# GpSimd's arithmetic in the weight stage moved to VectorE, in an attention and feed-forward kernel on one core

## The chip, the core and the metric

The kernel runs on one core of a Trainium2 chip. A core has engines that each work through their own queue of instructions in order: TensorE (PE in the profile; its weight loads are PEld), VectorE (DVE), ScalarE (ACT), GpSimd (POOL), and SyncE (SP), whose queue only issues transfers here. Engines wait for one another by semaphores. The time is that of one execution on the device in microseconds (us), the median of several.

## The reference

Four batches of 768 positions, 8 heads of width 64, all in fp32. Attention is local: position s sees the 8 first positions and its own last 96, with a bias that falls with distance by a slope per head.

```python
scores = scale * np.matmul(q, k.transpose(0, 1, 3, 2))
keep = is_global | is_local
scores = scores + bias[None, :, :, :]
scores = np.where(keep, scores, -1000000000.0)
a = np.exp(scores - np.max(scores, axis=-1, keepdims=True))
a = a / (np.sum(a, axis=-1, keepdims=True) + 1e-09)
x = np.matmul(a, v)                      # then (3072, 512): heads side by side
h = x @ w_in                             # w_in (512, 2048)
out = (h / (1.0 + np.exp(-h))) @ w_out   # w_out (2048, 512)
```

The two weight matrices come as 64-bit floats, so they are 16 MB in memory.

## The kernel before

**Split numbers.** Products are made from pairs. An fp32 value is rounded to a high part in a shorter format, and its low part is the value less the high part; a product is high x high + high x low + low x high. For the weights the high part is rounded on ScalarE (`conv_hi`, L387) and the low part subtracted (`conv_lo`, L391).

**Weights.** They come in 32 pieces (n = 0 to 31) of 128 partitions x 512 numbers, 512 KB each; even n are a 128-wide column slice of w_in for one f (f = n / 2, 16 in all), odd n the matching rows of w_out. A piece is loaded by SP (`stage`, L364) to a staging buffer. There are three of these; for n under 20 two of every five pieces use space that is lent by the last pieces' own place. Three VectorE steps put the 64-bit float's bits together as an fp32 (`conv1` L368, `conv2` L374, `conv3` L380), after which the staging buffer is free; then come `conv_hi` and `conv_lo`. The fp32 form `wf` has three buffers until `conv_lo` is through.

**Attention.** 24 blocks of 128 positions. Per block, keys and queries are turned by PE, split (L503 and L507, from block 6 on L476 and L487), and the part of the keys that the next block needs is copied on (`carry`, L514 and L516, on GpSimd). Each block has four pairs of heads: scores on PE (L528, later L500), bias and row maximum in one VectorE operation (L540), exponentials with their sum on ScalarE (L548), sum guarded and inverted (L555, L559), exponentials scaled by it (`norm`, L572 or L574), turned on PE (L583), moved to SBUF (L589), and multiplied with the values on PE (L603). The result is split again (L615, L618).

**Feed-forward.** Two blocks make a group of 256 tokens; there are 12 groups, g = 0 to 11. One unit is one (g, f): 12 matmuls with w_in (L723), tanh on ScalarE (L729), the gate on VectorE (L733), its high part on ScalarE (L737), its low part (L742), 6 matmuls with w_out (L749). Groups 0 and 1 run side by side while the weights come in, f after f; from group 2 on every weight is there, and attention of later blocks is mixed between the units.

**The order.** All engines' queues are written out by a planner when the kernel is built (`Plan.run`). Each operation is given to it with its engine, a cost in ns, a rank, what it needs and what buffers it holds. The planner walks through time and gives each engine that is free the lowest rank that is ready and has buffers. The order of every queue follows from these costs, so another engine or cost for one operation moves others too. Where PE would have nothing before a set time, the planner puts in small filler matmuls (L861).

**Which engine.** `conv_lo` is always on GpSimd. The table's `PL=4` puts a gate's low part on GpSimd for groups 0 and 1 and f under 4, eight in all. `NP=(16, 0)` puts the first head's scaling of each of the first 16 pairs of heads on GpSimd; `NA=(0, 0)` puts none on ScalarE. Everything else of these kinds is on VectorE.

Of the kernel before, what the change touches and what calls it, by code (L numbers as in the profile page):

```python
# [10 lines left out]
F32 = mybir.dt.float32  # L11
# [6 lines left out]
ALU = mybir.AluOpType  # L18
# [15 lines left out]

    C0=14, CR=1, LW=1, LB=5, QB=3.5, RI=0.1, RN=0, RP=0.2, RM=0, RV=1.2, RQ=0.1, RB=3, LK=-25, LAG=1,

    BP=(4, 3), NA=(0, 0), NP=(16, 0), PL=4, NX=20, CF=2, AHEAD=5, CN=4, I0=6, QS='ACT',
)


# [130 lines left out]
def attn_moe(ctx, tc, q, k, v, n_global, n_local, w_in, w_out, out):  # L171
    nc = tc.nc
# [3 lines left out]
    NHP = H // 2  # L176
# [52 lines left out]
    st = {}  # L229
# [83 lines left out]
    op = plan.op  # L313
    DVE = lambda n: 1000 * (62 + n) / 960
# [21 lines left out]
    for hp in range(NHP):  # L336
        for first in (True, False):
            p = hp >= PAR["BP"][first]
# [49 lines left out]

    def conv_lo(n):
        _, hi, lo = weights(n)  # L390
        nc.gpsimd.tensor_sub(lo, st["f", n], hi.bitcast(F32))  # L391

    o_w, o_l = [], [None, None]
    for n in range(2 * NFC):
        rank = PAR["C0"] + PAR["CR"] * n
        a, m, x = [] if lent(n) is not None else [Buf("big")], Buf("mid"), lent(n)
        o = op("DMA", 1456, rank - PAR["LW"], (lambda n=n: stage(n, "w")), [o_l[x]] if not a else (), a, PAR["DL"])
        o = op("DVE", 335, rank, (lambda n=n: conv1(n)), [o], [*a, m])
        o = op("DVE", 602, rank, (lambda n=n: conv2(n)), [o], [*a, m])
        o = op("DVE", 602, rank, (lambda n=n: conv3(n)), [o], [*a, m])  # L400
        if x is not None:
            o_l[x] = o
        o_wf = o
        hi = op("ACT", 520, rank, (lambda n=n: conv_hi(n)), [o] + (o_l if n >= 2 * NFC - 4 else []), [m])
        lo = op("POOL", 1225, rank, (lambda n=n: conv_lo(n)), [hi], [m])
        o_w.append((hi, lo))
    lo["caps"] = dict(pt=5)

# [149 lines left out]
        t = blk[i]  # L558
        nc.vector.reciprocal(t["inv", hp], t["inv", hp])  # L559

    def norm_on(u, a):

        return "ACT" if u < PAR["NA"][a] else "POOL" if u < PAR["NP"][a] else "DVE"

    def norm(i, hp, a):
        t = blk[i]
        x = t["p", hp][:, a, :cols(i)[1]]
        eng = norm_on(NHP * i + hp, a)
        if eng == "ACT":
            nc.scalar.mul(x, x, t["inv", hp][:, a:a + 1])  # L570
        elif eng == "POOL":
            nc.gpsimd.tensor_mul(x, x, t["inv", hp][:, a:a + 1].to_broadcast(x.shape))  # L572
        else:
            nc.vector.tensor_scalar(x, x, t["inv", hp][:, a:a + 1], None, ALU.mult)  # L574

    def turn_p(i, hp, tp):
        t = blk[i]
# [48 lines left out]
    for i in range(B * NJ):  # L626
# [51 lines left out]
        for hp in range(NHP):  # L678
            u = NHP * i + hp
            stacked = i >= PAR["I0"]  # L680
            s, pe, pt, tp = [Buf("s") for _ in range(1 if stacked else 2)], Buf("pe"), Buf("pt"), Buf("tp")
            ks = [kk[x] for x in ("KH", "KL", "QH", "QL") + (("R",) if stacked else ())]
            n = cols(i)[1]
            o = op("PE", 432 if stacked else 640, u,
                   (lambda i=i, hp=hp, s=s, f=stack_scores if stacked else scores: f(i, hp, s)),
                   [x for y, x in ob.items() if i or y[1] <= hp < y[1] + NHP // 2] + [before.get("s") if stacked else None], s + ks)
            before["s"] = o_s[u] = o
            if u == PAR["HU"]:
                o["hold"] = 1
            o_e = []  # L690
            for a in range(2):
                x = op("DVE", 318 if j else 210, u, (lambda i=i, hp=hp, a=a: top_of(i, hp, a)),
                       [o, o_b[j == 0, hp], before.get("top") if stacked and not a else None], [s[a % len(s)], pe])
                if not a:
                    before["top"] = x
                o_e.append(op("ACT", ACT(n, 112) + 186, u, (lambda i=i, hp=hp, a=a: expo(i, hp, a)), [x], [pe]))
            o = op("DVE", 67, u - PAR["RI"], (lambda i=i, hp=hp: guard(i, hp)), o_e, [pe])
            o = op("DVE", 72, u - PAR["RI"], (lambda i=i, hp=hp: inverse(i, hp)), [o], [pe])
            cost = dict(ACT=380, DVE=250, POOL=640) if j else dict(ACT=293, DVE=196, POOL=400)
            o = [op(norm_on(u, a), cost[norm_on(u, a)], u - PAR["RN"], (lambda i=i, hp=hp, a=a: norm(i, hp, a)), [o], [pe])  # L700
                 for a in range(2)]
            o = op("PE", 438 if j else 220, u - PAR["RP"], (lambda i=i, hp=hp, tp=tp: turn_p(i, hp, tp)), o, [pe, tp])
            o_m.append(op("ACT", ACT(512 if j else 256), u - PAR["RM"], (lambda i=i, hp=hp: move_p(i, hp)), [o, before.get("move") if stacked else None], [tp, pt]))
            before["move"] = o_m[-1]
            pts.append(pt)
            if not stacked or hp == NHP - 1:
                last = op("PE", ((1860 if j else 980) if stacked else 540 if j else 290), u - PAR["RV"],
                          (lambda i=i, hp=hp, av=pav: values_of(i, hp, av)),
                          [*o_m, last] + o_v, [*pts, pav, xb[g]["xh"], xb[g]["xl"], kk["vn"]] + ([kk["vp"]] if j else []))
                o_m, pts = [], []  # L710
# [27 lines left out]

    def moe_low(g, f):
        mo["gl", g, f] = gl = sb2.tile([P, GT], F32R, name="gl")  # L740
        eng = nc.gpsimd if g < 2 and f < PAR["PL"] else nc.vector
        eng.tensor_sub(gl, mo["th", g, f], mo["gh", g, f].bitcast(F32))  # L742

    def moe_o(g, f, tt, po):
        gh, gl, po = mo["gh", g, f], mo["gl", g, f], bank(po)
# [25 lines left out]
    for g in range(NGRP):  # L771
# [3 lines left out]
        for f in range(NFC):  # L775
            rank = 1e3 + (max(g, 1) * NFC + f + (PAR["LAG"] + 0.5 if g else 0))
            ph, th, gh, gl = Buf("h"), Buf("th"), Buf("gh"), Buf("gl")
            for c in range(NCC):
                o = op("PE", 329, rank + PAR["LK"] / 10, (lambda g=g, f=f, c=c, h=ph: moe_h(g, f, c, h)),
                       [o, *o_w[2 * f]] + o_x[g], [ph, xb[g]["xh"], xb[g]["xl"]])  # L780
                if f == c == 0:
                    o["hold"] = 2 if g == 1 else 1
            o_h[g, f] = o
            t = op("ACT", 264, FIRST + rank, (lambda g=g, f=f: moe_tanh(g, f)), [o], [ph, th])
            t = op("DVE", 335, FIRST + rank, (lambda g=g, f=f: moe_gate(g, f)), [t], [ph, th])
            hi = op("ACT", 307, FIRST + rank, (lambda g=g, f=f: moe_high(g, f)), [t], [th, gh])
            p = g < 2 and f < PAR["PL"]
            lo = op("POOL" if p else "DVE", 690 if p else 335, FIRST + rank, (lambda g=g, f=f: moe_low(g, f)), [hi], [th, gh, gl])
            for tt in range(NB):
                last[tt] = op("PE", 651, rank, (lambda g=g, f=f, tt=tt, x=po[tt]: moe_o(g, f, tt, x)),  # L790
                              [hi, lo, last[tt], *o_w[2 * f + 1]], [gh, gl, *po[tt:]])
                if g < 2 and f == NFC - 1:
                    last[tt]["hold"] = 1
# [243 lines left out]
```

## Time and profile before

| | |
|---|---|
| median of 3 runs | 757.61 us (755.15 to 757.96) |
| the profiled execution | 757.3 us, its span 755.5 us |
| mean granted TensorE clock | 0.992 |
| busy: PE, DVE, ACT, POOL | 721.3, 491.7, 422.6, 91.6 us |
| GpSimd's low parts of weights, L391 | 32 instructions, 47.5 us |
| GpSimd's scalings, L572 | 16, 9.1 us |
| GpSimd's low parts of gates, L742 | 8, 7.2 us |
| GpSimd's copies of keys, L514 and L516 | 80, 29.5 us |
| weight stage (first to last L368 to L380) | 32.8 to 144.9 us |

A row of the timeline gives the start in us, the length in us, the engine, the line in the kernel, the operation and the tiles (out<-in). Groups give count, busy us, mean ns of one, and the engine's idle time just before them with what ended it. A record's length runs from the start to the end of the instruction on its engine, so time in which it stood still after its start is inside.

### The profile page before, as it was taken

How to read it: one execution, taken by the hardware profiler on the slowest of the kernel's cores; microseconds unless marked ns; L12 is line 12 of the kernel's file. 1: busy time of each engine (PE TensorE's matmuls, PEld its weight loads, DVE VectorE, ACT ScalarE, POOL GpSimd, SP SyncE). 2: the span in 40 equal slices, each digit the busy share in tenths (PEclk: the TensorE clock that was granted, in tenths of full speed). 3: DMA queues.
4: the chain of work that ended last, by engine and by line, in shares of the span. 5: the costliest groups of instructions: out<-in, count | busy, mean ns of one | idle time of the engine just before them, and what ended most of it. 6: DMA issues, size and time to landing. Idle time of an engine off the chain costs nothing.

```text
span 755.5 us, 14215 instructions
## 1 busy us (share of the span) xinstructions
PE 721.3 (95%) x5203; PEld 636.8 (84%) x5203; DVE 491.7 (65%) x1439; ACT 422.6 (56%) x1105; POOL 91.6 (12%) x147
## 2 busy tenths in 40 slices
PE   8997676899999999999999999999999999999996
PEld 6776555788999999999899999998899999998995
DVE  5899999864666656756666757656666756544322
ACT  5976233574656656755656756646656646543221
POOL 3355545400000000000000000000000000000000
PEclk9999899999999999999999999999999999999999
DMA  7785535112412412313313324324314232000000
GB/s 148 214 211 175 163 121 183 56 29 54 132 62 69 118 60 71 102 49 97 99 49 90 87 52 109 85 54 109 97 31 109 71 82 54 29 2 1 29 1 33
DMA packets 117501, 63.98 MB, mean 85 GB/s; under 512 B 93744, under 2 KB 110384, under 8 KB 117424
## 3 DMA queue, kind: packets, MB, share of 16 engines
q1 hardware_dynamic: 116992, 62.86, 30.5%
q8 instruction: 43, 0.70, 0.4%
q14 instruction: 34, 0.28, 0.1%
q10 hardware_dynamic: 432, 0.13, 0.1%
HBM read 56.69 MB, written 6.29 MB: 83 GB/s over the span
## 4 chain that ended last, share of the span: by engine, by line
PE 83%; DVE 12%; issue 3%; DMA 1%; ACT 0%; SPq 0%; DVEq 0%
PE bank L723 33%; PE bank L749 32%; PE bank L603 5%; PE bank L583 4%; PE bank L500 4%; DVE wf L368 3%; PE bank L448 3%; DVE wf L374 2%; DVE wf L380 2%; DVE pe L540 1%; PE bank L861 1%; DVE pe L574 1%; PE bank L528 1%; DVE th L733 1%; DMA qn<-in_q_dram 1%
## 5 line engine op out<-in xcount | busy, mean ns | idle before, releaser
L723 PE MATMUL bank<-xh,WIH 128*128 128x256 f32 x768 | 226.2, 295 | 17.4 <-DVE th L733 16.1
L723 PE MATMUL bank<-xl,WIH 128*128 128x256 f32 x768 | 217.0, 283 | 0.0
L723 PE MATMUL bank<-xh,WIL 128*128 128x256 f32 x768 | 216.0, 281 | 0.0
L723 PEld LDWEIGHTS bank<-xh,WIH 128*128 128x128 f32 x768 | 145.2, 189 | 33.0 <-DVE th L733 22.3
L723 PEld LDWEIGHTS bank<-xl,WIH 128*128 128x128 f32 x768 | 145.4, 189 | 5.8
L723 PEld LDWEIGHTS bank<-xh,WIL 128*128 128x128 f32 x768 | 145.8, 190 | 0.0
L749 PE MATMUL bank<-WOH,gh 128*128 128x512 f32 x336 | 137.6, 410 | 0.0
L749 PE MATMUL bank<-WOH,gl 128*128 128x512 f32 x336 | 134.2, 399 | 2.7 <-DVE gl L742 2.7
L749 PE MATMUL bank<-WOL,gh 128*128 128x512 f32 x336 | 133.1, 396 | 0.0
L729 ACT ACTIVATE th<-bank 128x256 f32<-128x256 f32 x192 | 73.7, 384 | 101.1 <-PE bank L723 98.2
L737 ACT CAST gh<-th 128x256 fp32r<-128x256 f32 x192 | 77.3, 403 | 92.6 <-PE bank L749 55.0
L733 DVE SCALAR_TENSOR_TENSOR th<-th,bank 128x256 f32<-128x256 f32 x192 | 80.3, 418 | 64.4 <-ACT th L729 62.7
L742 DVE TENSOR_TENSOR gl<-th,gh 128x256 fp32r<-128x256 f32 x184 | 80.4, 437 | 54.1 <-ACT gh L737 51.8
L540 DVE CUSTOM_DVE_ANT_0 pe<-bank,B 128x232 f32<-128x232 f32 (+1 forms) x192 | 69.7, 376 | 62.8 <-PE bank L500 54.9
L548 ACT ACTIVATE pe<-pe,NM 128x232 f32<-128x232 f32 (+1 forms) x192 | 90.5, 473 | 22.9 <-DVE NM L540 21.1
L749 PEld LDWEIGHTS bank<-WOH,gl 128*128 128x128 f32 x336 | 63.6, 189 | 21.3 <-DVE gl L742 6.0
L589 ACT COPY pt<-bank 128x512 f32<-128x512 f32 (+1 forms) x96 | 52.4, 549 | 45.2 <-PE bank L583 44.2
L749 PEld LDWEIGHTS bank<-WOL,gh 128*128 128x128 f32 x336 | 64.3, 191 | 6.4
L749 PEld LDWEIGHTS bank<-WOH,gh 128*128 128x128 f32 x336 | 64.3, 191 | 6.3 <-issue 0.3
L514 POOL CAST KH<-KH 128x32 fp32r<-128x32 f32 x20 | 4.5, 227 | 458.5 <-PE bank L500 449.9
L583 PE MATMUL bank<-ident,pe 128*128 128x128 f32 (+1 forms) x352 | 55.3, 275 | 3.5 <-DVE th L733 2.5
L574 DVE TENSOR_SCALAR pe<-pe,rs 128x232 f32<-128x232 f32 (+1 forms) x176 | 53.9, 342 | 1.1
(112 smaller groups left out, 1008.2 us busy)
## 6 DMA issues: line engine op xcount, KB each, us to landing
c<-in_moe_w_in_dram SPq DMA_DIRECT2D x16, 512.0 KB, 4.0
c<-in_moe_w_out_dram SPq DMA_DIRECT2D x16, 512.0 KB, 4.3
vn<-in_v_dram SPq DMA_DIRECT2D x24, 256.0 KB, 3.4
w<-in_moe_w_in_dram SPq DMA_DIRECT2D x12, 512.0 KB, 4.8
w<-in_moe_w_out_dram SPq DMA_DIRECT2D x12, 512.0 KB, 3.6
kn<-in_k_dram SPq DMA_DIRECT2D x23, 256.0 KB, 3.0
qn<-in_q_dram SPq DMA_DIRECT2D x23, 256.0 KB, 3.2
out_dram<-osb SPq DMA_DIRECT2D x23, 256.0 KB, 3.2
```

Of the source, the lines that this page charges most:

```text
L540: nc.vector.tensor_tensor_reduce(t["p", hp][:, a, :n], t["s", hp][a][:, :n], B1[:, h] if i % NJ else B0[:, h], -SC, 3.0e38, ALU.add, ALU.m ...
L548: nc.scalar.activation(x, x, AF.Exp, bias=NM[:, i * H + h:i * H + h + 1], scale=-1.0, accum_out=t["sum", hp][:, a:a + 1],)
L574: nc.vector.tensor_scalar(x, x, t["inv", hp][:, a:a + 1], None, ALU.mult)
L583: nc.tensor.transpose(ps[:n, c, a], pe[:, a, c0:c0 + n], ident)
L589: nc.scalar.copy(t["pt", hp][:, c], t["tp", hp][:, c])
L603: nc.tensor.matmul(pav[r, hp], x[:, 2 * hp + a], pt[:P if c else C1, c, a], start=not c or not i % NJ, stop=c == 1,)
L723: nc.tensor.matmul(ph, w[:, c, fs], x[:, c], start=not c and not n, stop=c == NCC - 1 and n == 2)
L729: nc.scalar.activation(th, mo["ph", g, f], AF.Tanh, scale=0.5)
L733: nc.vector.scalar_tensor_tensor(gf, gf, 1.0, mo["ph", g, f], ALU.add, ALU.mult)
L737: nc.scalar.copy(gh, mo["th", g, f])
L742: eng.tensor_sub(gl, mo["th", g, f], mo["gh", g, f].bitcast(F32))
L749: nc.tensor.matmul(po, a[:, s], w_o(w, f), start=f == 0 and n == 0, stop=f == NFC - 1 and n == 2)
```

## The change

The table's entries `NA`, `NP` and `PL` go. `conv_lo`, every scaling of exponentials and every low part of a gate are issued on VectorE, and the planner gets VectorE's costs for them. GpSimd keeps the set-up of the first 15 us and the copies of keys.

```diff
-    BP=(4, 3), NA=(0, 0), NP=(16, 0), PL=4, NX=20, CF=2, AHEAD=5, CN=4, I0=6, QS='ACT',
+    BP=(4, 3), NX=20, CF=2, AHEAD=5, CN=4, I0=6, QS='ACT',
...
     def conv_lo(n):
         _, hi, lo = weights(n)
-        nc.gpsimd.tensor_sub(lo, st["f", n], hi.bitcast(F32))
+        nc.vector.tensor_sub(lo, st["f", n], hi.bitcast(F32))
...
-        lo = op("POOL", 1225, rank, (lambda n=n: conv_lo(n)), [hi], [m])
+        lo = op("DVE", 602, rank, (lambda n=n: conv_lo(n)), [hi], [m])
...
-    def norm_on(u, a):
-
-        return "ACT" if u < PAR["NA"][a] else "POOL" if u < PAR["NP"][a] else "DVE"
-
     def norm(i, hp, a):
         t = blk[i]
         x = t["p", hp][:, a, :cols(i)[1]]
-        eng = norm_on(NHP * i + hp, a)
-        if eng == "ACT":
-            nc.scalar.mul(x, x, t["inv", hp][:, a:a + 1])
-        elif eng == "POOL":
-            nc.gpsimd.tensor_mul(x, x, t["inv", hp][:, a:a + 1].to_broadcast(x.shape))
-        else:
-            nc.vector.tensor_scalar(x, x, t["inv", hp][:, a:a + 1], None, ALU.mult)
+        nc.vector.tensor_scalar(x, x, t["inv", hp][:, a:a + 1], None, ALU.mult)
...
-            cost = dict(ACT=380, DVE=250, POOL=640) if j else dict(ACT=293, DVE=196, POOL=400)
-            o = [op(norm_on(u, a), cost[norm_on(u, a)], u - PAR["RN"], (lambda i=i, hp=hp, a=a: norm(i, hp, a)), [o], [pe])
+            o = [op("DVE", 250 if j else 196, u - PAR["RN"], (lambda i=i, hp=hp, a=a: norm(i, hp, a)), [o], [pe])
                  for a in range(2)]
...
     def moe_low(g, f):
         mo["gl", g, f] = gl = sb2.tile([P, GT], F32R, name="gl")
-        eng = nc.gpsimd if g < 2 and f < PAR["PL"] else nc.vector
-        eng.tensor_sub(gl, mo["th", g, f], mo["gh", g, f].bitcast(F32))
+        nc.vector.tensor_sub(gl, mo["th", g, f], mo["gh", g, f].bitcast(F32))
...
-            p = g < 2 and f < PAR["PL"]
-            lo = op("POOL" if p else "DVE", 690 if p else 335, FIRST + rank, (lambda g=g, f=f: moe_low(g, f)), [hi], [th, gh, gl])
+            lo = op("DVE", 335, FIRST + rank, (lambda g=g, f=f: moe_low(g, f)), [hi], [th, gh, gl])
```

In the changed file the lines stand a little higher: gate L722, its low part L730, matmuls of a unit L712 and L737, scaling L564, fillers L848; L364 to L391 are as before.

The order on VectorE late in the weight stage, before, around pieces 27 to 29 (`wf_27` is the fp32 form of piece 27, `th` a gate, `gl` its low part):

```order
L368 TENSOR_SCALAR wf_27_1553<-w_27_1510 128x512
L374 SCALAR_TENSOR_TENSOR wf_27_1553<-w_27_1510,wf_27_1553 128x512
L742 TENSOR_TENSOR gl_1570<-th_1545,gh_1560 128x256
L380 SCALAR_TENSOR_TENSOR wf_27_1553<-w_27_1510,wf_27_1553 128x512
L368 TENSOR_SCALAR wf_28_1578<-w_28_1542 128x512
L733 SCALAR_TENSOR_TENSOR th_1576<-th_1576,bank0_82 128x256
L374 SCALAR_TENSOR_TENSOR wf_28_1578<-w_28_1542,wf_28_1578 128x512
L368 TENSOR_SCALAR wf_29_1597<-w_29_1555 128x512
L742 TENSOR_TENSOR gl_1602<-th_1576,gh_1591 128x256
L380 SCALAR_TENSOR_TENSOR wf_28_1578<-w_28_1542,wf_28_1578 128x512
```

And now, around the same pieces:

```order
L374 SCALAR_TENSOR_TENSOR wf_27_1735<-w_27_1683,wf_27_1735 128x512
L722 SCALAR_TENSOR_TENSOR th_1758<-th_1758,bank2_84 128x256
L380 SCALAR_TENSOR_TENSOR wf_27_1735<-w_27_1683,wf_27_1735 128x512
L368 TENSOR_SCALAR wf_28_1770<-w_28_1728 128x512
L730 TENSOR_TENSOR gl_1778<-th_1758,gh_1765 128x256
L374 SCALAR_TENSOR_TENSOR wf_28_1770<-w_28_1728,wf_28_1770 128x512
L391 TENSOR_TENSOR WOL_80<-wf_27_1735,WOH_79 128x512
L722 SCALAR_TENSOR_TENSOR th_1791<-th_1791,bank2_84 128x256
L380 SCALAR_TENSOR_TENSOR wf_28_1770<-w_28_1728,wf_28_1770 128x512
L368 TENSOR_SCALAR wf_29_1803<-w_29_1746 128x512
L730 TENSOR_TENSOR gl_1811<-th_1791,gh_1801 128x256
L374 SCALAR_TENSOR_TENSOR wf_29_1803<-w_29_1746,wf_29_1803 128x512
```

The low part of piece 27 (L391) now stands between the second and third conversion steps of piece 28, and a gate with its low part comes in every piece. Counted over the queue, the old order has 20 gates (L733) ahead of the third conversion step of the last piece, the new one 27 (L722).

The order on GpSimd in the weight stage, before:

```order
L514 CAST KL_822<-KL_645 128x4x8
L516 CAST KL_822<-KL_645 128x4x96
L391 TENSOR_TENSOR WOL_80<-wf_3_832,WOH_79 128x512
L742 TENSOR_TENSOR gl_956<-th_920,gh_951 128x256
L391 TENSOR_TENSOR WIL_78<-wf_4_841,WIH_77 128x4x128
L742 TENSOR_TENSOR gl_1014<-th_972,gh_1004 128x256
L391 TENSOR_TENSOR WOL_80<-wf_5_967,WOH_79 128x512
```

And now:

```order
L514 CAST KL_815<-KL_652 128x4x8
L516 CAST KL_815<-KL_652 128x4x96
L514 CAST KH_2188<-KH_1045 128x4x8
L516 CAST KH_2188<-KH_1045 128x4x96
L514 CAST KL_2194<-KL_1054 128x4x8
```

After the copies for block 5 GpSimd's next work is the copies for block 7. On PE the new order has 98 fillers in place of 65, all ahead of the sixth unit's first matmul.

## The prediction, on record before the result was known

> **What bounds the kernel now.** I read the page's shares first, then the page's 40 slices.
>
> ```profile
> span 755.5 us, 14215 instructions
> PE 721.3 (95%) x5203; PEld 636.8 (84%) x5203; DVE 491.7 (65%) x1439; ACT 422.6 (56%) x1105; POOL 91.6 (12%) x147
> DVE  5899999864666656756666757656666756544322
> POOL 3355545400000000000000000000000000000000
> ```
>
> TensorE (PE) at 95% looks like the bound, and VectorE (DVE) with 65% like an engine with room. The slices say otherwise for the first fifth: from slice 2 to slice 6 (38 to 132 us) DVE is at 9, and just there GpSimd (POOL) works at 4 to 5 tenths. Stretches of 20 us (length; then busy time of PE, PEld, DVE, ACT, POOL, with counts; clock, DMA share, GB/s):
>
> ```profile
> 60.00:80.00 20.00, 13.41 (x84) 11.09 (x83) 19.74 (x36) 10.84 (x24) 11.17 (x9) 1.00 0.58 179
> 80.00:100.00 20.00, 16.10 (x75) 12.86 (x75) 19.93 (x26) 7.01 (x15) 10.11 (x9) 0.83 0.54 159
> 100.00:120.00 20.00, 12.86 (x72) 9.64 (x72) 19.93 (x29) 6.58 (x15) 10.30 (x7) 1.00 0.42 131
> 160.00:180.00 20.00, 20.00 (x131) 18.00 (x130) 9.93 (x29) 10.44 (x26) 0.00 (x0) 1.00 0.12 28
> ```
>
> With weights coming in, PE does 72 to 84 matmuls in 20 us; after them, 131. So the kernel has two bounds: DVE until about 145 us, PE from then on. The list of waits agrees on who is late:
>
> ```profile
> PE bank L723 <- DVE th L733: 16.1, 10, 3.0
> ```
>
> The question is therefore what one step of the DVE queue costs in the weight stage. The timeline, DVE alone, then the GpSimd instruction of that time:
>
> ```profile
> 46.36 0.16 DVE L555 TENSOR_SCALAR rs<-sm 128x2 f32<-128x2 f32 x1
> 46.43 0.68 DVE L380 SCALAR_TENSOR_TENSOR wf<-w,wf 128x512 uint32<-128x512 uint32 x1
> 47.03 0.15 DVE L559 RECIPROCAL rs<-rs 128x2 f32<-128x2 f32 x1
> 47.11 0.38 DVE L540 CUSTOM_DVE_ANT_0 pe<-bank,B 128x232 f32<-128x232 f32 x1
> ...
> 47.41 0.33 DVE L574 TENSOR_SCALAR pe<-pe,rs 128x232 f32<-128x232 f32 x1
> 47.66 0.39 DVE L540 CUSTOM_DVE_ANT_0 pe<-bank,B 128x232 f32<-128x232 f32 x1
> ...
> 47.98 0.68 DVE L507 TENSOR_TENSOR KL<-bank,KH 128x512 fp32r<-128x512 f32 x1
> 48.58 1.58 DVE L368 TENSOR_SCALAR wf<-wl 128x512 uint32<-128x512 uint32 x2
> ```
> ```profile
> 105.18 0.41 DVE L733 SCALAR_TENSOR_TENSOR th<-th,bank 128x256 f32<-128x256 f32 x1
> 105.51 0.68 DVE L374 SCALAR_TENSOR_TENSOR wf<-wl,wf 128x512 uint32<-128x512 uint32 x1
> 106.11 1.51 DVE L368 TENSOR_SCALAR wf<-w 128x512 uint32<-128x512 uint32 x1
> 107.54 0.68 DVE L380 SCALAR_TENSOR_TENSOR wf<-wl,wf 128x512 uint32<-128x512 uint32 x1
> 108.14 0.41 DVE L742 TENSOR_TENSOR gl<-th,gh 128x256 fp32r<-128x256 f32 x1
> 108.48 0.68 DVE L374 SCALAR_TENSOR_TENSOR wf<-w,wf 128x512 uint32<-128x512 uint32 x1
> ```
> ```profile
> 105.98 1.35 POOL L391 TENSOR_TENSOR WIL<-wf,WIH 128x512 fp32r<-128x512 f32 x1 [1.61 <-ACT WIH L387]
> ```
>
> From start to start a conversion step (L374, L380) or a 128x512 subtraction takes 0.60 us, the scaling of exponentials (L574) 0.25, the score step (L540) 0.32, a gate (L733) 0.33, a gate's low part (L742) 0.34, the small ones 0.07. But the first conversion step L368 at 106.11 is recorded with 1.51 us: GpSimd's subtraction had begun at 105.98 and ended at 107.33, 1.22 us after DVE's start, which leaves 0.29 for the work. Without GpSimd beside it the record is 0.41 long (below, 32.77): the rest was waiting. The gate reads one operand from PSUM; none of the 31 gates before 180 us is longer than 0.42, whatever GpSimd did. So two engines that seem to work in parallel take turns.
>
> **The change part by part.**
>
> *What goes.* The DVE groups of 40 to 145 us, different shapes apart (count, busy us, mean ns):
>
> ```profile
> L380 DVE SCALAR_TENSOR_TENSOR wf<-w,wf 128x512 uint32<-128x512 uint32 x23 | 22.8, 993 | 0.1
> L368 DVE TENSOR_SCALAR wf<-w 128x512 uint32<-128x512 uint32 x22 | 20.1, 914 | 0.0
> L374 DVE SCALAR_TENSOR_TENSOR wf<-w,wf 128x512 uint32<-128x512 uint32 x23 | 18.8, 816 | 0.3
> L374 DVE SCALAR_TENSOR_TENSOR wf<-wl,wf 128x512 uint32<-128x512 uint32 x8 | 7.5, 933 | 0.0
> L742 DVE TENSOR_TENSOR gl<-th,gh 128x256 fp32r<-128x256 f32 x12 | 7.1, 594 | 0.0
> L368 DVE TENSOR_SCALAR wf<-wl 128x512 uint32<-128x512 uint32 x8 | 7.0, 887 | 0.0
> L380 DVE SCALAR_TENSOR_TENSOR wf<-wl,wf 128x512 uint32<-128x512 uint32 x8 | 6.9, 866 | 0.0
> L574 DVE TENSOR_SCALAR pe<-pe,rs 128x232 f32<-128x232 f32 x11 | 5.3, 513 | 0.0
> ```
>
> Each mean less its undisturbed length (0.41 for L368 and L742, 0.68 for L374 and L380, 0.33 for L574), times the count: 7.2 + 11.1 + 3.1 + 2.0 + 2.2 + 3.8 + 1.5 + 2.0 = 32.9 us of DVE standing still behind GpSimd. A second way gives the same. The DVE stream from the first conversion to the end of the last one is, undisturbed, by the counts of the order before: 32 x (0.335 + 0.605 + 0.605) for the conversions, 18 score steps x 0.32, 10 pairs of small ones x 0.14, 14 scalings x 0.25, 9 subtractions of 128x512 x 0.605, 20 gates x 0.33, 12 low parts x 0.335. That is 49.4 + 5.8 + 1.4 + 3.5 + 5.4 + 6.6 + 4.0 = 76.1 us. The trace has
>
> ```profile
> 32.77 0.41 DVE L368 TENSOR_SCALAR wf<-w 128x512 uint32<-128x512 uint32 x1
> 144.21 0.68 DVE L380 SCALAR_TENSOR_TENSOR wf<-w,wf 128x512 uint32<-128x512 uint32 x1
> ```
>
> so 144.9 - 32.8 = 112.1 us, 36 more than the work. With DVE at 19.9 of 20 that is no idling.
>
> *What comes.* The same stretch in the new order holds 31 low parts of weights (L391), 27 gates, 27 low parts of gates, 20 scalings, and the rest as before. The trace has no L391 on DVE. Nearest are L507 (same shape, one operand in PSUM, 0.60) and L742 (both operands in SBUF, 256 wide, 0.34, so about 0.61 at 512); bounds 0.41 (the one-operand L368) and 0.68; I take 0.605. Added: 31 x 0.605 + 7 x 0.33 + 15 x 0.335 + 6 x 0.25 = 18.8 + 2.3 + 5.0 + 1.5 = 27.6 us, stream 103.7. Ahead of the first conversion 10 more scalings come to DVE (2.3 us), where its second slice is at 8 tenths; some of its waits behind GpSimd go there too: +1. The copies of keys stay on GpSimd (L514, L516; eight between 33 and 52 us, 0.2 to 0.7 each): +1 for waits behind them. Last conversion done: 32.8 + 1 + 103.7 + 1 = 138.5 us if DVE never waits for others.
>
> The Trainium skill speaks against counting from start to start: "VectorE: DVE Perf Modes", section "Terms", says that the pipeline is drained after every operation and the next can't issue until it is empty. By that each added instruction would cost its whole recorded length, some 0.075 more for 59, so 4.4 us. The rows above disagree: 46.43 + 0.68 is 47.11, and the next begins at 47.03.
>
> *New waits.* A low part now stands in DVE's queue and waits for ScalarE's rounding of the same weight; behind it stand the next conversions and gates. By the steps above the new order puts 0.8 to 2.3 us of other DVE work between a weight's last conversion and its low part. The rounding of weights and of gates on ScalarE in 40 to 145 us:
>
> ```profile
> L387 ACT CAST WIH<-wf 128x512 fp32r<-128x512 f32 x15 | 9.3, 620 | 15.1 <-DVE wf L380 14.9
> ...
> L737 ACT CAST gh<-th 128x256 fp32r<-128x256 f32 x20 | 8.1, 404 | 10.8 <-DVE th L733 8.8 <-PE bank L749 1.9
> ```
>
> 0.62 us, covered unless a gate's rounding (0.40) is ahead of it on ScalarE. The other cover is thinner. From weight 23 on there are three staging buffers, and a load is issued when DVE has left the buffer. The new order leaves 3.5 to 6.6 us (median 5.6) between that and the first conversion that needs the load, and loads take, from issue to landing in 60 to 145 us,
>
> ```profile
> w<-in_moe_w_in_dram SPq DMA_DIRECT2D x9, 512.0 KB, 3.8
> w<-in_moe_w_out_dram SPq DMA_DIRECT2D x9, 512.0 KB, 3.6
> ```
>
> so one or two of nine come late, by under 1 us. For these, and for gates that wait on PE, I take 4 us in all, bounds 0 and 12. Last conversion done: 142.5 us.
>
> *What it is worth.* From there on PE is the bound, so what counts is how much of its work is then left. One unit (one group, one f) costs PE
>
> ```profile
> 174.69 0.28 PE L723 MATMUL bank<-xh,WIH 128*128 128x256 f32 x1
> 177.50 0.28 PE L723 MATMUL bank<-xh,WIH 128*128 128x256 f32 x1
> ```
>
> 2.81 us, these being the first matmuls of two units in a row. At the last conversion the old order has had 20 gates, the new one 27: 7 units less remain, 19.7 us. Attention stands at the same place in both (18 score steps in the stretch). Can PE do 27 units by then? They are 76 us of the stretch's 109, and attention of a little over two blocks is at most 9 us each (what 192 units of 2.81 leave of the span, over 24 blocks): some 96 of 109. In the second half the new order asks for one unit per 3.1 us of DVE work, so PE is at nine tenths. Together: 144.9 - 142.5 + 19.7 = 22.1 us. The profiled execution took 757.3 us by the device's clock, near the median of 757.61 of the runs; 757.3 - 22.1 = 735.2, and I say **735.5 us**. The 33 fillers (L861, then L848) that the new order adds to PE stand before the sixth unit, where PE has gaps; they cost nothing there.
>
> **The rivals.**
>
> *DVE, in order, now waits for its suppliers* (faster, but by half). For: the staging distances of 3.5 us stand below the 3.8 of a landing, and ScalarE is shared by three roundings. Against: before, all of these were late because of DVE, and DVE idled 0.1 us before L380. Every load from weight 23 on late by 1.3 us is 9 x 1.3 = 12; time 735.5 + 11 = 746.5.
>
> *Nothing waits* and the stages around gain as well: 4 us less, and the copies cost nothing: 730. PE's granted clock was 0.83 in 80 to 100 us, beside its pauses; without pauses another 2: 728.
>
> *Whole lengths count* (the drain): 735.5 + 4.4 = 740. Against it: the starts above.
>
> *The long records are DVE's own work* on buffers that DMAs fill, and GpSimd only happens to be there: slower. Then nothing goes and 27.6 us come on the queue that bounds the stage: 755.5 + 27.6 - 19.7 + 1 = 764.4 of span, 766. It decides once more than some 22 of the 33 us stay. Against: L368 has 0.41 or 1.51 on the same buffers, by whether GpSimd is in L391.
>
> *It does not show*: the time gained in the stage goes to a wait of the same size on PE's side: 757. Against: PE's 72 matmuls in 20 us against 131.
>
> **How the numbers follow.** Forecast 0.70, suppliers 0.14, nothing waits 0.06, drain 0.03, no change 0.04, slower 0.03. Faster by over 0.5% (under 753.8; 0.5% is about what a measurement of this kernel tells from no change): 0.93; within: 0.04; slower: 0.03. The range goes from "nothing waits" to just above "suppliers": 727 to 748.
>
> **What would show it.** Right: L368 at 0.41, L374 and L380 at 0.68 in the mean; L391 on DVE near 0.68; GpSimd idle but for copies; DVE still at 9 tenths until about 142 us; the last conversion there with 27 gates before it; PE full from 140 us on. Wrong: DVE with gaps before L368 (loads) or L391 (ScalarE) of over 10 us in the sum; L368 still near 0.9 without GpSimd; or PE idling before gates as now.

## The result and the profile after

The changed kernel takes 736.18 us (median of 4 runs, 735.29 to 736.54), the one before beside it 757.35 us: a ratio of 0.9724, 95% interval 0.9702 to 0.9746, so 21.2 us less. The profiled execution has a span of 733.8 us against 755.5. Its page, the same lines as shown of before:

```profile
span 733.8 us, 14225 instructions
PE 718.7 (98%) x5236; PEld 635.5 (87%) x5236; DVE 481.4 (66%) x1495; ACT 422.4 (58%) x1105; POOL 28.8 (4%) x91
DVE  5899999867667467565665665665666656544332
POOL 2110000000000000000000000000000000000000
```

VectorE (DVE) is at 9 tenths in the same slices as before, GpSimd (POOL) only copies keys. VectorE's busy time went down by 10 us although 56 instructions of GpSimd's came to it: before, its records contained time in which it stood still. The groups of the weight stage (33 to 146 us, different shapes apart) show it:

```profile
L374 DVE SCALAR_TENSOR_TENSOR wf<-w,wf 128x512 uint32<-128x512 uint32 x24 | 16.2, 682 | 0.1
L380 DVE SCALAR_TENSOR_TENSOR wf<-w,wf 128x512 uint32<-128x512 uint32 x24 | 16.2, 680 | 0.0
L730 DVE TENSOR_TENSOR gl<-th,gh 128x256 fp32r<-128x256 f32 x29 | 12.1, 417 | 0.9 <-ACT gh L726 0.8
L391 DVE TENSOR_TENSOR WIL<-wf,WIH 128x512 fp32r<-128x512 f32 x16 | 10.9, 683 | 0.0
L368 DVE TENSOR_SCALAR wf<-w 128x512 uint32<-128x512 uint32 x24 | 9.9, 417 | 0.3 <-DMA w<-in_moe_w_in_dram 0.3
```

L380 went from 993 to 680 ns in the mean, L374 from 816 to 682, L368 from 914 to 417, a gate's low part from 594 to 417. The stage ends earlier, and TensorE (PE) gets more work in it. The stretches of 20 us, and TensorE's wait for gates:

```profile
60.00:80.00 20.00, 19.66 (x126) 16.45 (x125) 19.76 (x52) 12.65 (x31) 0.00 (x0) 1.00 0.52 155
80.00:100.00 20.00, 19.24 (x116) 15.65 (x115) 20.00 (x43) 9.48 (x22) 0.00 (x0) 1.00 0.67 198
100.00:120.00 20.00, 18.86 (x117) 15.59 (x117) 19.93 (x43) 8.91 (x20) 0.00 (x0) 1.00 0.46 143
```
```profile
PE bank L712 <- DVE th L722: 3.0, 6, 0.7
```

116 to 126 matmuls in 20 us where there were 72 to 84; the wait for gates fell from 16.1 us to 3.0.

TensorE's own account closes the sum, since in both kernels it is what ends last. Time without an instruction on TensorE: 755.5 - 721.3 = 34.2 us before, 733.8 - 718.7 = 15.1 now, 19.1 less. Fillers, small matmuls that stand where TensorE would otherwise have nothing, from the groups of before and of the change:

```profile
L861 PE MATMUL bank<-wx 128*128 128x256 bf16 x65 | 12.6, 336 | 2.1 <-DVE wx L307 1.1 <-DVE QL L507 0.8 <-DVE NM L540 0.3
```
```profile
L848 PE MATMUL bank<-wx 128*128 128x256 bf16 x98 | 18.0, 310 | 1.1 <-DVE wx L307 1.1
```

5.4 us more. All other matmuls: 721.3 - 12.6 = 708.7 before, 718.7 - 18.0 = 700.7 now, 8.0 less (the mean granted clock went from 0.992 to 0.999, and the 0.83 of 80 to 100 us is now 1.00; by these means the clock is some 5 of the 8, an estimate, and what it is worth by itself no run separates). 19.1 - 5.4 + 8.0 = 21.7 us, the difference of the spans.

### The profile page after: what moved, and what is told of

It reads as the page before. It is cut to its first block, busy times and chain, and to the rows that moved or that the text cites. A ratio compares the mean times of both kernels' runs of the same rounds, so it can differ in the third digit from the quotient of the medians.

```text
span 733.8 us, 14225 instructions
## 1 busy us (share of the span) xinstructions
PE 718.7 (98%) x5236; PEld 635.5 (87%) x5236; DVE 481.4 (66%) x1495; ACT 422.4 (58%) x1105; POOL 28.8 (4%) x91
## 4 chain that ended last, share of the span: by engine, by line
PE 87%; DVE 8%; DMA 2%; ACT 1%; issue 1%; SPq 0%; DVEq 0%; ACTq 0%
PE bank L712 33%; PE bank L737 33%; PE bank L593 6%; PE bank L573 5%; PE bank L500 4%; PE bank L448 3%; DVE wf L374 2%; PE bank L528 2%; PE bank L848 2%; DVE wf L380 1%; DVE th L722 1%; DVE gl L730 1%; DMA c<-in_moe_w_in_dram 1%; DVE wf L368 1%; DMA qn<-in_q_dram 1%
## 5 line engine op out<-in xcount | busy, mean ns | idle before, releaser
L712 PE MATMUL bank<-xh,WIH 128*128 128x256 f32 x768 | 225.3, 293 | 3.1 <-DVE th L722 3.0
L712 PE MATMUL bank<-xl,WIH 128*128 128x256 f32 x768 | 216.1, 281 | 0.5 <-DVE xl L608 0.5
L712 PE MATMUL bank<-xh,WIL 128*128 128x256 f32 x768 | 215.1, 280 | 0.0
L712 PEld LDWEIGHTS bank<-xh,WIH 128*128 128x128 f32 x768 | 144.5, 188 | 19.0 <-DVE th L722 10.3
L712 PEld LDWEIGHTS bank<-xl,WIH 128*128 128x128 f32 x768 | 144.7, 188 | 6.4 <-DVE xl L608 0.7
L712 PEld LDWEIGHTS bank<-xh,WIL 128*128 128x128 f32 x768 | 144.8, 189 | 0.0
L737 PE MATMUL bank<-WOH,gh 128*128 128x512 f32 x336 | 136.4, 406 | 0.0
L737 PE MATMUL bank<-WOH,gl 128*128 128x512 f32 x336 | 132.4, 394 | 0.0
L737 PE MATMUL bank<-WOL,gh 128*128 128x512 f32 x336 | 132.2, 393 | 0.0
L722 DVE SCALAR_TENSOR_TENSOR th<-th,bank 128x256 f32<-128x256 f32 x192 | 80.2, 418 | 59.2 <-ACT th L718 57.7
L730 DVE TENSOR_TENSOR gl<-th,gh 128x256 fp32r<-128x256 f32 x192 | 81.3, 424 | 51.2 <-ACT gh L726 49.1
L737 PEld LDWEIGHTS bank<-WOH,gl 128*128 128x128 f32 x336 | 63.0, 187 | 15.5 <-DVE gl L730 0.2
L737 PEld LDWEIGHTS bank<-WOH,gh 128*128 128x128 f32 x336 | 63.4, 189 | 6.8 <-issue 0.7
L737 PEld LDWEIGHTS bank<-WOL,gh 128*128 128x128 f32 x336 | 63.4, 189 | 6.1
L564 DVE TENSOR_SCALAR pe<-pe,rs 128x232 f32<-128x232 f32 (+1 forms) x192 | 55.9, 330 | 0.9
L573 PEld LDWEIGHTS bank<-ident,pe 128*128 128x128 f32 (+1 forms) x352 | 41.4, 136 | 10.3 <-DVE pe L564 3.0
```

The lines of the kernel that those rows point to most:

```text
L573: nc.tensor.transpose(ps[:n, c, a], pe[:, a, c0:c0 + n], ident)
L712: nc.tensor.matmul(ph, w[:, c, fs], x[:, c], start=not c and not n, stop=c == NCC - 1 and n == 2)
L722: nc.vector.scalar_tensor_tensor(gf, gf, 1.0, mo["ph", g, f], ALU.add, ALU.mult)
L730: nc.vector.tensor_sub(gl, mo["th", g, f], mo["gh", g, f].bitcast(F32))
L737: nc.tensor.matmul(po, a[:, s], w_o(w, f), start=f == 0 and n == 0, stop=f == NFC - 1 and n == 2)
```

## The experiments

The theory: GpSimd's instructions that read operands make VectorE's stand still; without them the VectorE stream is as long as its steps, and its earlier end and the units done by then make the gain. The rivals: the new order of the queues makes the gain, not the absence of GpSimd; any work on GpSimd slows VectorE; it is one of the three kinds of work that matters. All ratios are to the kernel before, measured beside each. "Last conversion" is the third step (L380) of the last piece, a gate counts as ahead of it if it starts earlier, and both are read from each kernel's trace.

| kernel | last conversion ends, us | gates ahead of it | 27th gate, us | time, us | ratio (95%) |
|---|---|---|---|---|---|
| before | 144.9 | 20 | 167.4 | 757.35 | |
| the change | 139.7 | 27 | 136.7 | 736.18 | 0.9724 (0.9702 to 0.9746) |
| weights' low parts alone | 138.5 | 29 | 131.9 | 728.32 | 0.9618 (0.9602 to 0.9634) |
| ... and low parts of gates | 139.1 | 27 | 136.1 | 732.47 | 0.9671 (0.9655 to 0.9687) |
| ... and scalings | 142.4 | 29 | 134.1 | 732.52 | 0.9674 (0.9658 to 0.9690) |
| small work alone | 145.7 | 21 | 163.9 | 755.42 | 0.9983 (0.9972 to 0.9994) |
| old order, all on VectorE | 134.4 | 20 | 156.5 | 746.17 | 0.9855 (0.9838 to 0.9871) |
| new order, work on GpSimd | 152.6 | 27 | 149.1 | 747.26 | 0.9859 (0.9832 to 0.9886) |
| the change, GpSimd reading | 158.1 | 27 | 154.3 | 759.18 | 1.0021 (1.0008 to 1.0034) |
| the change, GpSimd writing | 140.0 | 27 | 136.9 | 739.77 | 0.9770 (0.9750 to 0.9789) |
| weights, more small work left | 135.0 | 26 | 137.4 | 735.60 | 0.9719 (0.9700 to 0.9739) |
| weights, dearer units | 137.1 | 26 | 139.5 | 738.01 | 0.9742 (0.9714 to 0.9770) |

### The order and the engine, one at a time

*The old order, with the three kinds of work issued on VectorE.* The planner is told the old engines and costs, so every queue but the two keeps its order; only the issuing engine differs:

```diff
 def conv_lo(n):
-    nc.gpsimd.tensor_sub(lo, st["f", n], hi.bitcast(F32))
+    nc.vector.tensor_sub(lo, st["f", n], hi.bitcast(F32))
...
 def norm(i, hp, a):
...
-    elif eng == "POOL":
-        nc.gpsimd.tensor_mul(...)
...
 def moe_low(g, f):
-    eng = nc.gpsimd if g < 2 and f < PAR["PL"] else nc.vector
-    eng.tensor_sub(...)
+    nc.vector.tensor_sub(...)
```

> All three kinds run on VectorE as in the change, but the planner still reckons with GpSimd and its costs, so that the order of all other work is the old one: 20 gates ahead of the last conversion, 99.1 us of steps. Stream theory: last conversion at 33 + 99 + 2 = 134 us, 11 us earlier than before, with as many gates as before: about 746 us, half of the gain. Rival, the lock alone makes the gain: 736. Rival, the order alone makes it: 757.

Measured 746.17 us. The last conversion and the wait for gates in its trace:

```profile
133.69 0.68 DVE L380 SCALAR_TENSOR_TENSOR wf<-w,wf 128x512 uint32<-128x512 uint32 x1
```
```profile
PE bank L721 <- DVE th L731: 12.3, 13, 1.7
```

VectorE's steps grow by 23 us, to 99.1, and yet it is through 10.5 us earlier, and the whole gains 11. The standing still that went (36 us by the prediction's second way) less the 23 us of work that came would make 13; 10.5 were found.

*The other half alone: the change's plan, with the work issued on GpSimd as before.*

```diff
-        nc.vector.tensor_sub(lo, st["f", n], hi.bitcast(F32))
+        nc.gpsimd.tensor_sub(lo, st["f", n], hi.bitcast(F32))
...
+        if NHP * i + hp < 16 and not a:
+            nc.gpsimd.tensor_mul(x, x, t["inv", hp][:, a:a + 1].to_broadcast(x.shape))
...
-        nc.vector.tensor_sub(gl, mo["th", g, f], mo["gh", g, f].bitcast(F32))
+        (nc.gpsimd if g < 2 and f < 4 else nc.vector).tensor_sub(...)
```

> The reverse: the planner reckons as in the change and the order is the new one (27 gates ahead of the last conversion), but the same three kinds of work run on GpSimd as before: 80.8 us of steps on VectorE, and about 33 us of waits behind GpSimd. Stream theory: last conversion at 33 + 81 + 33 = 147 us with 27 gates done, so 757 + 2 - 20 = 740 us: most of the gain without taking anything off GpSimd. Rival, the lock makes the gain and the order only goes with it: 755 or more, since the order was made for another engine. Rival, the order alone: 736.

Measured 747.26 us, about halfway between the expectations' 740 and 755. The groups of 33 to 150 us, and the last conversion:

```profile
L380 DVE SCALAR_TENSOR_TENSOR wf<-w,wf 128x512 uint32<-128x512 uint32 x23 | 20.8, 912 | 0.0
L733 DVE TENSOR_TENSOR gl<-th,gh 128x256 fp32r<-128x256 f32 x18 | 13.6, 758 | 0.1
```
```profile
151.94 0.68 DVE L380 SCALAR_TENSOR_TENSOR wf<-w,wf 128x512 uint32<-128x512 uint32 x1
```

The instructions are again far above their undisturbed lengths, and the last conversion ends at 152.6 us: 7.7 later than before, and 5.6 later than the expected 147, since VectorE also idles for 6.4 us in the stage, mostly ahead of gates whose tanh is late. But 27 gates go ahead of it, and the kernel is 10 us faster all the same: the gates done by then outweigh the later end. So the gain of 21 has two halves: the order gives 10, with GpSimd in the way or without it, and VectorE's freedom 11, in either order.

### Which of the three kinds of work

*The weights' low parts alone* on VectorE, the small work left on GpSimd (`NP` and `PL` as before):

```diff
-        nc.gpsimd.tensor_sub(lo, st["f", n], hi.bitcast(F32))
+        nc.vector.tensor_sub(lo, st["f", n], hi.bitcast(F32))
...
-        lo = op("POOL", 1225, rank, (lambda n=n: conv_lo(n)), [hi], [m])
+        lo = op("DVE", 602, rank, (lambda n=n: conv_lo(n)), [hi], [m])
```

> Of the three moves only the weights' low parts go to VectorE (cost 602 in the planner); the first heads' scalings and the first eight gates' low parts stay on GpSimd. The new order has 29 gates ahead of the last conversion and 100.6 us of undisturbed VectorE steps from the first conversion on. Stream theory (time follows from the length of the VectorE stream, waits behind GpSimd included, and from the gates done in it): some 4 us of waits behind the small GpSimd work stay, last conversion at about 138 us, 730 to 737 us: all of the gain. If the scalings and gates mattered as much: above 745.

728.32 us: 29 us better than before, 8 us better than the change, and better than any theory had it. *The small work alone* (`NP=(0, 0)`, `PL=0`, L391 on GpSimd as before):

> The other two moves alone: scalings and gates' low parts on VectorE, the weights' low parts stay on GpSimd. 21 gates ahead of the last conversion, 81.0 us of steps. Stream theory: about 29 us of waits behind the weights' low parts stay, last conversion at about 144 us, 753 to 758 us: little or nothing gained. Rival, that any GpSimd arithmetic less is worth its share of the 47.5 + 9.1 + 7.2 us: about 752 by share.

755.42 us, as expected: GpSimd's low parts of weights go on holding VectorE, and L380 is at 1035 ns. Then the small kinds one by one on top of the weights' low parts: the gates' (`PL=0`),

> The weights' and the first eight gates' low parts on VectorE, the first heads' scalings stay on GpSimd as before the change. 27 gates ahead of the last conversion, 102.3 us of steps. Stream theory: as the change less 1.5 us of steps, 733 to 736 us. Rival, the scalings on VectorE are what makes the change slower than the weights alone: 728.

and the scalings (`NP=(0, 0)`),

> The weights' low parts and all scalings on VectorE, the first eight gates' low parts stay on GpSimd. 29 gates ahead of the last conversion, 103.7 us of steps, of which 0.9 are attention that comes earlier. Stream theory: as the change by its steps, but two gates more done, so 736 - 5.6 = 730 us, and if attention done earlier counts 729. Rival, the scalings are what makes the change slower: 735.

732.47 and 732.52 us, a little better than expected in the first case and 2.5 us worse in the second: each costs 4.2 us, and both together (the change) 7.9. The low parts of the weights give all of the gain and more.

Where the 8 us lie is seen by the gates (the two traces are 7.3 us apart). The 10th is at 83.57 us with the weights alone and at 83.90 in the change; the 27th at 131.91 and 136.73; the 50th at 220.55 and 225.93. VectorE with the weights alone, late in the stage, and then in the change:

```profile
101.01 0.42 DVE L733 SCALAR_TENSOR_TENSOR th<-th,bank 128x256 f32<-128x256 f32 x1
101.34 0.69 DVE L380 SCALAR_TENSOR_TENSOR wf<-wl,wf 128x512 uint32<-128x512 uint32 x1
101.94 0.42 DVE L368 TENSOR_SCALAR wf<-wl 128x512 uint32<-128x512 uint32 x1
102.28 0.42 DVE L742 TENSOR_TENSOR gl<-th,gh 128x256 fp32r<-128x256 f32 x1
102.62 0.69 DVE L374 SCALAR_TENSOR_TENSOR wf<-wl,wf 128x512 uint32<-128x512 uint32 x1
103.22 0.68 DVE L391 TENSOR_TENSOR WIL<-wf,WIH 128x512 fp32r<-128x512 f32 x1
103.82 0.42 DVE L733 SCALAR_TENSOR_TENSOR th<-th,bank 128x256 f32<-128x256 f32 x1
```
```profile
105.71 0.41 DVE L722 SCALAR_TENSOR_TENSOR th<-th,bank 128x256 f32<-128x256 f32 x1
106.04 0.75 DVE L368 TENSOR_SCALAR wf<-w 128x512 uint32<-128x512 uint32 x2
106.71 0.68 DVE L391 TENSOR_TENSOR WOL<-wf,WOH 128x512 fp32r<-128x512 f32 x1
107.31 0.41 DVE L730 TENSOR_TENSOR gl<-th,gh 128x256 fp32r<-128x256 f32 x1
107.65 1.28 DVE L374 SCALAR_TENSOR_TENSOR wf<-w,wf 128x512 uint32<-128x512 uint32 x2
108.85 0.41 DVE L722 SCALAR_TENSOR_TENSOR th<-th,bank 128x256 f32<-128x256 f32 x1
```

One piece and one gate with its low part are 0.335 + 0.605 + 0.605 + 0.605 + 0.33 + 0.335 = 2.815 us of VectorE, and one unit is 2.81 us of TensorE: the two are even. With the weights alone, gates start every 2.81 us, and TensorE is full:

```profile
100.00:120.00 20.00, 20.00 (x131) 18.14 (x131) 20.00 (x43) 9.91 (x21) 0.00 (x0) 1.00 0.44 134
```

In the change there are 3.14 us between the two gates shown, since steps of two pieces stand between them (x2). From the 10th to the 27th gate its VectorE starts 19 first steps, 19 second, 19 third ones and 19 low parts for 17 gates; with the weights alone it is 17, 18, 17 and 17. That is 0.67 + 0.605 + 1.21 + 1.21 = 3.7 us of work ahead of need, of the 4.5 us that the same 17 gates take longer. With the weights alone these steps stand behind the gates, where TensorE has work anyway. The kernel with the gates' low parts moved has the same counts as the change, 19 of each for 17 gates in 52.7 us; the one with the scalings moved has 17 of each in 48.5 us, and is 2.0 us behind already at its 10th gate, for a reason that the runs do not show. The change loses another 1.9 us after the 50th gate (507.9 us from there to the end against 506.0), of which 1.3 are a pause of TensorE at 356 us, ahead of matmuls that wait for scalings (L564). The change and the three runs on its plan have such pauses after 200 us, of 1.3 to 3.0 us together; the kernel before, the old order on VectorE and the weights alone have none. What in the plan makes them stays open.

*More of the small work on GpSimd* would, if this were all, help further (weights' low parts on VectorE, `NP=(20, 0)`, `PL=8`):

> The low parts of the weights on VectorE as in the change, but GpSimd keeps more of the small work than before the change: 20 of the scalings (NP=20 for 16) and 16 low parts of gates (PL=8 for 4). The steps on VectorE from the first to the last conversion fall to 94.9 us (100.6 with weights alone moved, 103.7 in the change), but only 26 gates stand ahead of the last conversion (29 and 27). Theory A (both terms count: the last conversion's time, and 2.3 us of TensorE work for each unit by then): last conversion at about 133 to 135 us, three units fewer than with weights alone, so 727 to 732. Rival B (the small work on GpSimd holds VectorE as the weights' low parts did): last conversion not before 138, 735 to 738. Rival C (whatever leaves VectorE helps, by 4 us for each eight or sixteen as in the runs with gates or scalings moved): 722 to 725.

735.60 us. Theory A has the last conversion right, 135.0 us; rival B has the time. The profiled execution was the fastest of four, 732.7 us, and for it theory A's sum is nearly right: 726.6 - 3.5 + 3 x 2.3 = 730.0 us of span, 731.0 measured (2.3 us is what one gate more was worth in the change, 16.0 us for 7, worked out below). What the other three executions have on top of it no trace shows. GpSimd is in VectorE's way until 110 us. The groups of 33 to 146 us, GpSimd's and VectorE's:

```profile
L742 POOL TENSOR_TENSOR gl<-th,gh 128x256 fp32r<-128x256 f32 x16 | 17.9, 1116 | 36.4 <-ACT gh L737 36.1 <-POOL pe L572 0.3
```
```profile
L391 DVE TENSOR_TENSOR WIL<-wf,WIH 128x512 fp32r<-128x512 f32 x16 | 12.2, 760 | 0.0
L391 DVE TENSOR_TENSOR WOL<-wf,WOH 128x512 fp32r<-128x512 f32 x14 | 11.1, 795 | 0.0
```

A low part of 128x256 takes 1.12 us there and 0.42 on VectorE, with L391 up from 683. TensorE gets 101 to 108 matmuls per 20 us from 60 to 120 us. Eight low parts on GpSimd came out better than none and better than sixteen, each with the order that the planner made for it (29, 27 and 26 gates ahead of the last conversion); the number of instructions alone was not tested.

*A planner that is told the unit's true price* (weights' low parts alone; a unit is 4 x 353 + 2 x 701 ns = 2.81 us to it, and was 4 x 329 + 2 x 651 = 2.62):

```diff
-    o = op("PE", 329, rank + PAR["LK"] / 10, (lambda g=g, f=f, c=c, h=ph: moe_h(g, f, c, h)),
+    o = op("PE", 353, rank + PAR["LK"] / 10, (lambda g=g, f=f, c=c, h=ph: moe_h(g, f, c, h)),
...
-    last[tt] = op("PE", 651, rank, (lambda g=g, f=f, tt=tt, x=po[tt]: moe_o(g, f, tt, x)),
+    last[tt] = op("PE", 701, rank, (lambda g=g, f=f, tt=tt, x=po[tt]: moe_o(g, f, tt, x)),
```

> Weights' low parts alone on VectorE, and the planner is given TensorE costs of 353 and 701 ns in place of 329 and 651, so that a unit costs it the 2.81 us that the trace has (2.62 before). VectorE's steps up to the last conversion 98.6 us, 26 gates ahead of it, against 100.6 and 29. Theory A (last conversion plus 2.3 us for each unit not yet done): last conversion at 136 to 137, three units fewer, 730 to 734. Rival (an order planned with the true cost has fewer waits everywhere): below 727.

738.01 us: both expectations are wrong, the rival's sign too. 26 gates ahead of a last conversion at 137.1 make a span of 726.6 - 1.5 + 3 x 2.3 = 732 by theory A; it is 736.0. Of the other 4 us, 3 lie after the 50th gate (509.0 us from there to the end, 506.0 with the weights alone), and their cause stays open. A truer cost is no safe way to a better order here.

### What holds VectorE

The change, and on GpSimd beside each low part of a weight three subtractions of 128x128 that read the same two tiles; nobody reads their result:

```diff
         nc.vector.tensor_sub(lo, st["f", n], hi.bitcast(F32))
+        for c in range(3):
+            x, y = ...                                   # 128 columns of wf and of the high part
+            nc.gpsimd.tensor_sub(st["scr"], x, y)
```

> The change, with three more subtractions of 128x128 on GpSimd per piece of the weights, from the same two tiles as VectorE's low part into a small tile that nobody reads. VectorE's and TensorE's order is that of the change. Lock theory (a VectorE instruction with two operands in SBUF, or in its fast one-operand form, stands still while GpSimd works on SBUF): three times 0.4 us of holding per piece, mostly met by some such instruction, so 20 to 33 us of waits on VectorE, 755 to 768 us, L374, L380 and L391 well above 0.68 in the mean, L722 still 0.41. Rival, the waits before came from what depended on GpSimd's results (buffers, late weights): nothing depends here, 736 to 738 us.

And the change with work on GpSimd that writes only: a copy of one column, to hold it to its place, and six memsets of 128x128 that nobody reads:

```diff
+        nc.gpsimd.tensor_copy(st["scr"][:, :1], x)       # one column of wf
+        for _ in range(6):
+            nc.gpsimd.memset(st["scr"], 0.0)
```

> As the run before, but GpSimd copies one column from the piece and then fills a 128x128 tile with zeros six times: about 1.3 us of GpSimd per piece that writes SBUF and hardly reads it. If any work of GpSimd on SBUF holds VectorE: 755 to 768 us as with the reads. If what is shared is the reading side alone: L374, L380, L391 stay near 0.68, only L368 and L564 (fast one-operand form, which may also need the writing side) may lengthen; 736 to 745 us.

The readers cost 23 us and undo all of the gain (759.18), the writers 3.6 (739.77), though GpSimd is busy with 63.6 us of reading in the one and 43.7 us of memsets in the other. Groups of the weight stage, with readers and with writers, then GpSimd's own:

```profile
L380 DVE SCALAR_TENSOR_TENSOR wf<-w,wf 128x512 uint32<-128x512 uint32 x24 | 18.6, 780 | 0.0
L391 DVE TENSOR_TENSOR WIL<-wf,WIH 128x512 fp32r<-128x512 f32 x16 | 14.4, 898 | 0.0
L727 DVE SCALAR_TENSOR_TENSOR th<-th,bank 128x256 f32<-128x256 f32 x27 | 11.0, 409 | 0.1
```
```profile
L380 DVE SCALAR_TENSOR_TENSOR wf<-w,wf 128x512 uint32<-128x512 uint32 x24 | 16.2, 681 | 0.0
L391 DVE TENSOR_TENSOR WIL<-wf,WIH 128x512 fp32r<-128x512 f32 x16 | 10.9, 682 | 0.0
```
```profile
L396 POOL TENSOR_TENSOR scr<-wf,WIH 128x128 f32<-128x128 f32 x48 | 32.0, 667 | 30.4 <-ACT WIH L387 27.5
```
```profile
L397 POOL MEMSET scr<- 128x128 f32 x192 | 43.7, 228 | 11.1
```

What VectorE reads from two tiles in SBUF is held by readers (L380 by 100 ns, L391 by 215 in the mean) and not by writers (1 ns or less); the gate, which has one operand in PSUM, is held by neither. The Trainium skill says this in "SBUF — State Buffer", section "Who interferes with whom": a VectorE instruction with two inputs in SBUF contends with a GpSimd instruction that reads SBUF, not with one that only writes it. The two runs agree, with these numbers.

A rival is that VectorE waits for a buffer which GpSimd still reads. With the readers it takes 124.6 us from its first to its last conversion, 17.8 more than in the change, and idles for 0.6 us of that, none of it for GpSimd: the instructions themselves are longer.

The 3.6 us of the writers are not in the stage. The last conversion is at 140.0 us against 139.7, the 50th gate at 225.97 against 225.93. TensorE then pauses for 1.2 us between 520 and 540 us, and the span ends some 2 us later behind its last matmul than in the change. Why, when the memsets are long over, the runs do not show. The readers' trace has the same: of the 22.7 us between it and the change's 18.3 are there by the 50th gate (244.22), the rest comes behind it, 2 us of it behind the last matmul. So the reading itself costs some 18 us, a little under the 20 to 33 us of waits that were expected.

## Why the prediction was right

The forecast was 735.5 us, in a range of 727 to 748; 736.18 was measured. Point by point:

*What VectorE stood still for.* Right. Without GpSimd's arithmetic L380, L374 and L368 are at their undisturbed lengths, and L391 on VectorE has 683 ns where 0.68 was said. The price of a step from start to start (0.605) was right too: the steps of the stretch are 103.7 us, and from 32.90 us to the end of the row

```profile
139.07 0.68 DVE L380 SCALAR_TENSOR_TENSOR wf<-w,wf 128x512 uint32<-128x512 uint32 x1
```

it is 106.8. VectorE idles for 1.4 us of that, 1.0 of it in the three waits named below. Steps that took longer from start to start than reckoned are another 1.6 us: L368 by 0.6 (353 ns in the mean for 335), the scalings and the small steps of attention by 0.8, where one of each stands beside a copy of keys on GpSimd with 0.2 to 0.3 us more than its usual length. The rival "whole lengths count" falls by the same rows: the L391 at 106.71 lasts until 107.39, and the next instruction starts at 107.31. The Trainium skill's drain ("VectorE: DVE Perf Modes", section "Terms") is not seen as time between these instructions.

*New waits: too large.* 4 us were put on waits for ScalarE and loads (bounds 0 and 12). About 1 came in waits of any size: 0.31 us for a rounding, 0.37 for a tanh, 0.3 for a load. With the +1 on the start of the stage, which came at 32.90 and not 33.8, the last conversion ended at 139.7 and not 142.5: 2.8 us better than forecast. The rival "suppliers late" falls by this: all loads together held VectorE for 0.3 us. (Its price was not worked out cleanly either: 12 us in place of the 4 make 743.5, not the 746.5 given.)

*What it is worth: too large by about as much.* 7 units of 2.81 us were to remain less after the last conversion, 19.7 us. The 34th gate stands in the traces of before and of the change at

```profile
192.55 0.42 DVE L733 SCALAR_TENSOR_TENSOR th<-th,bank 128x256 f32<-128x256 f32 x1 [0.16 <-ACT th L729]
```
```profile
171.46 0.42 DVE L722 SCALAR_TENSOR_TENSOR th<-th,bank 128x256 f32<-128x256 f32 x1
```

so from the last conversion to there it is 192.55 - 144.89 = 47.7 us before and 171.46 - 139.75 = 31.7 now: 16.0 us, 3.7 short. Two things were left out. In that stretch TensorE did 156 of the first matmuls of units (L723) before and 84 (L712) now, which is 6 units less and not 7: a gate ahead of the last conversion is not a whole unit done. And two blocks of attention stand there with fewer units to fill the gaps; TensorE isn't full:

```profile
160.00:165.00 5.00, 4.82 (x32) 3.55 (x30) 3.68 (x11) 4.68 (x16) 0.00 (x0) 1.00 0.59 156
165.00:170.00 5.00, 4.63 (x39) 4.63 (x40) 3.30 (x12) 4.09 (x9) 0.89 (x4) 1.00 0.86 213
170.00:175.00 5.00, 4.56 (x32) 3.91 (x31) 3.46 (x14) 4.41 (x14) 0.38 (x1) 1.00 0.51 146
```

"PE full from 140 us on" was wrong by the 1.0 us that is missing in these 15, of which 0.5 lie ahead of the 34th gate.

The sum: 5.1 us by the earlier last conversion (2.4 forecast), 16.0 by the units (19.7), 0.6 in the rest; 21.7 against 22.1. Two terms were off by about 3 to 4 us each way, and the forecast is as close as it is because they cancel: that closeness is luck, the mechanism is not.

The form of the sum holds well beyond this pair. Take the span, less the end of the last conversion, plus 2.3 us for each gate ahead of it: before and the change give 656.6 and 656.2, and seven of the other ten traces 654.6 to 656.7. The exceptions are the dearer units (658.7) and the two with added work on GpSimd (659.6 and 660.6), whose excess lies after the 50th gate.

*Fillers.* "They cost nothing there" is neither shown nor refuted. They take 5.4 us more of TensorE in all and last until 57.0 us (42.9 before). No delay of a unit shows: the first gate came at 47.22 us, before at 50.09, and with the weights alone, where the 72 fillers end at 49.5 us, the 10th gate is only 0.3 us earlier than in the change.

*What the prediction did not ask.* It took the three kinds of work as one, by what they add to VectorE's stream. The runs give the weights' low parts all of the gain; each small kind, 1.7 and 3.1 us in VectorE's steps up to the last conversion, cost 4.2. The sum that the prediction was built on has both in it: against the weights alone, the gates' low parts end the last conversion 0.5 us later with 2 gates less (0.5 + 2 x 2.3 = 5.1; the spans differ by 5.1), the scalings 3.9 us later with the same 29 (3.9; the spans differ by 3.8). It was worked out for the whole change only, and not for its parts.

## What to carry to other kernels

Read the length of one instruction beside what GpSimd does at that moment: where it changes with that, the engines take turns, and the work can go to the engine that does it faster. Then move only what holds the other engine for long: the subtractions that held VectorE for up to 1.1 us each paid, the 24 small instructions did not. And where an order is planned from costs, count what the new order puts ahead of the point where the bound passes from one engine to the other: half of this gain was order. Work out the sum for each part of a change by itself, too: the best kernel here was a part of it.

## What the runs showed of the hardware

- GpSimd waits too. Beside VectorE's stream its copy of one column (128x1), in the run with writers, is recorded with 638 ns in the mean of 32: ten have 183 to 187 ns, the longest 1.79 us.

```profile
L395 POOL COPY scr<-wf 128x1 f32<-128x1 f32 x32 | 20.4, 638 | 32.2 <-DVE wf L380 28.5 <-DVE rs L565 2.4
```

- The one-operand conversion step L368, which GpSimd's subtraction had held for over a microsecond, has 469 ns in the mean beside the added reads, and 432 beside the added writes, for 417 in the change: what writes do to it is small here.
- A subtraction of 128x512 takes 0.68 us on VectorE and 1.28 to 1.81 on GpSimd (32 in before, 1.48 in the mean, its own waiting included): work that went to GpSimd to relieve VectorE could hold it longer than the work itself would have taken there.
